# Two layers of attention and gated mixing on one core: transposes moved to transfers, VectorE's exponentials rebuilt from two addends

## The chip, the core and the metric

The kernel runs on one core of a Trainium2 chip. Five engines work side by side, each through its own list of instructions in order: TensorE (PE in the profile, with PEld for the loading of its weights), VectorE (DVE), ScalarE (ACT), GpSimd (POOL) and SyncE (SP), which here only issues transfers. They meet at semaphores. Matrix products land in PSUM, eight banks of 128 x 512 float32; everything else lives in SBUF, 128 partitions wide. The metric is the time on the device in microseconds (us), the median of several runs.

## The reference

Two identical layers are applied to x, 2048 tokens by 512 channels in bfloat16:

```python
x = x + attention(layernorm(x))
x = x + mixer(layernorm(x))
```

Attention has 32 query heads of 16 channels and one shared key and value head: `softmax(q k^T / 4) v`, then a 512 x 512 output product. The scores of one layer are 32 x 2048 x 2048 numbers, and each goes through an exponential. The mixer computes `z = gelu(x w_in)`, 1792 channels wide, keeps the first half as z1, normalises the second half to z2, mixes z2 over tokens with the 2048 x 2048 matrix `w_sp`, adds a bias per token, multiplies by z1 and applies `w_out`. `w_sp` is needed transposed, with source tokens on the partitions.

## The kernel before, in words

The 2048 tokens are 16 tiles of 128. Attention is cut into 32 groups per layer (`GROUPS`): two token tiles with 16 heads, or, for the last two tiles, one tile with 32 heads. A group goes over the 16 key tiles; one (group, key tile) pair is a unit. A unit has four blocks of 128 keys x 512 columns: four products on TensorE with 32 rows each (`scores`, L800) that can run beside each other. A layer has 512 units and so 2048 blocks.

Most units go to ScalarE. Their blocks fill two PSUM slots in turn, one of three banks and one of two (`push_slot`); one ScalarE instruction takes the exponential of a whole slot into the ring `P_ring` (L824), and TensorE multiplies each block by the values, with a column of ones for the softmax's sum (L841). All units of a group add up in one bank (`PVB`), which VectorE empties at the group's end (L926 to L935). The first two query tiles' four groups go over the keys piece by piece as these come (`attn_first`), the other 28 groups over all 16 key tiles at once (`attn_rest`).

Some units go to VectorE (`push_unit_dve`). It adds a bias to the scores, which are scaled to units of 1/128 of a binary exponent, clips them at zero and converts them to 16-bit integers (L872, four times a unit, 128 x 512 each). Read as bfloat16, such an integer is a power of two with a straight-line fraction. The error of that line is averaged away with five tables: the integers plus four constants (L881, four times a unit, 128 x 2048), and five weighted value products on TensorE (L887, five times four). `ON_DVE` gives three such units to each of 20 groups and two to each of 8, `FIRST_DVE` one to each of the first four groups: 80 a layer, 160 in all. The five tables of a unit lie in a ring of six tiles (`big`).

The order of every engine is made before the run by a planner (`_Graph.schedule`): each operation has a cost, a latency and a priority, and a simulated run picks what is ready. The result is one fixed list for each engine, the SP queue of transfers too. Where TensorE would lie idle the planner puts in products that add zero or write to a free bank (L631, L636, L639).

Three things are transposed before their products. Normalised tokens `xn` (`ln_tiles`) and attention outputs `o_norm` (`turn_o`, `turn_tile`) are turned on TensorE against an identity (L721, L945, L955) and copied out of PSUM by VectorE (L725, L948, L958). `w_sp` is read once at the start in 16 strips, turned on TensorE (L1272), copied (L1275) and written to a scratch tensor in HBM (`turn_wsp`); `mix_stage` and `mix_late` fetch pieces of it from there (L1154, L1189), 16 times a layer. The weights `wo`, `w_in`, `w_out` are loaded between these strips.

The mixing sums of early source tokens are formed during attention, in two stages, kept in HBM (`gp_scratch`) and read again. At the layer's end `mix_late` adds the last four source tiles, multiplies by z1 and applies `w_out`. At the change of layers the keys come in pieces of 2, 2, 4, 4 and 4 tiles (`KEYS`), each as soon as its tokens are done, and the first 16 units need only the first four key tiles. Three lines say what is queued in which way:

```python
def dma(fn, r, w, chan, us):
    return op("sp", fn, 0.7, r=r, w=w, prio=5, lat=us, chan=chan)
KEYS = ((0, 2), (2, 2), (4, 4), (8, 4), (12, 4))
```

Of the kernel before, what the change touches and what calls it, by code (L numbers as in the profile page):

```python
# [20 lines left out]
NF1 = 7  # L21
# [6 lines left out]
NPH = 5  # L28
PH_A = (0, 26, 51, 77, 102)
PH_W = (0.828125, 0.71875, 0.625, 0.54296875, 0.47460938)  # L30
Q_SCALE = 128.0 * 1.4426950408889634 * 0.25
E_SCALE = 0.6931471805599453 / 128.0
PH_BIAS = 127.0 * 128.0 - 128.0 * 2.102375911
# [7 lines left out]
BESIDE = 0.03  # L41

HOLDS = 2.5

# [31 lines left out]
class _Op:  # L76
    __slots__ = ("eng", "fn", "dur", "lat", "prio", "seq", "deps", "succ", "nleft", "chan", "chan_val",
                 "inc", "pos", "val", "clock", "t0", "task", "mode", "rows", "work", "opens", "nstart", "due", "chain")

    def __init__(self, eng, fn, dur, lat, prio, seq, chan, task, mode):  # L80
# [8 lines left out]
        self.lat = lat  # L89
        self.prio = prio  # L90
# [16 lines left out]
class _Graph:  # L107
# [66 lines left out]
    def schedule(self):  # L174
# [154 lines left out]
        while True:  # L329
            moved = True  # L330
            while moved:
                moved = False
                for e in ENGS:
                    if free[e]:
# [25 lines left out]
                        push(now + us + o.lat + SEM_LAT, 1, o)  # L360
                        at = now + us + o.lat + SEM_LAT
# [11 lines left out]
            while ev and ev[0][0] <= now + 1e-9:  # L373
                _, _, what, x = heapq.heappop(ev)
                if what == 0:
                    free[x] = True
                elif what == 1:
                    for s, k in x.succ:
                        if k == 1:
                            met(s, x)  # L380
                    t = x.task
                    if t is not None:
                        t.left -= 1
                        if t.left == 0:
                            for b in t.banks:
                                bank_free[b] = True
# [75 lines left out]
def bass_interleave_layers__grouped_kv_mqa__mixer_gmlp__prompt_kernel(  # L462
# [15 lines left out]
    P = 128  # L478
# [82 lines left out]
    z1flat = z1c[:].rearrange("p f s -> p (f s)")  # L561
    wsp_stage = z1flat[:, 0:2 * S].rearrange("p (b s) -> p b s", b=2)
    wsp_tile = z1flat[:, 2 * S:4 * S].rearrange("p (b t q) -> p b t q", b=2, q=P)
    Z1ALL = [("z1", f, t) for f in range(NF1) for t in range(NT)]

    wspT_d = nc.dram_tensor("wspt_scratch", [NT, P, S], BF16)
    wspT_dv = wspT_d.ap().rearrange("st p t -> p st t")
# [19 lines left out]
    def dma(fn, r, w, chan, us):  # L587
        return op("sp", fn, 0.7, r=r, w=w, prio=5, lat=us, chan=chan)

    def dve(fn, us, r, w, prio=5):  # L590
        return op("dve", fn, us, r=r, w=w, prio=prio)
# [73 lines left out]
    def load_weights(i):  # L665

        rd = [("wd", 2 * i + 1)]
        if i == 0:
            dma(lambda e: e.dma_start(wo_r[:], A_wo.rearrange("(c p) n -> p c n", p=P)), rd, ["wo"], "wo", 6.0)
        elif i == 1:  # L670
            dma(lambda e: e.dma_start(w_in_r[:], B_w_in.rearrange("(kd p) f -> p kd f", p=P)), rd, ["w_in"], "win", 10.0)
        elif i == 2:
            dma(lambda e: e.dma_start(w_out_r[:], B_w_out.rearrange("(c p) n -> p c n", p=P)), rd, ["w_out"], "wout",
                10.0)
# [29 lines left out]
    def ln_tiles(t0, n, xT, keys, per_tile, prio=5):  # L704
# [13 lines left out]
        while t < t0 + n:  # L718
            m = 1 if per_tile else min(2, t0 + n - t)
            tk = _Task()  # L720
# [3 lines left out]
            c0 = (t if xT is xnTA else t % CT) * P  # L724
# [78 lines left out]
    def push_slot(n):  # L803
# [22 lines left out]
        main["last"] = op("act", act_e, 0.065 + n * 0.4267, r=[tk], w=[("P", s0 + k) for k in range(n)], prio=3)  # L826
# [32 lines left out]
    def push_unit_dve(u):  # L859
# [3 lines left out]
        tiles = [phr["base"] + (phr["n"] + a) % phr["ring"] for a in range(NPH)]  # L863
        phr["n"] += NPH
        first_op = None
        for j in range(4):
# [7 lines left out]
                0.66, [tk], BIG(tiles[0]) if j == 0 else [("phj", tiles[0], j)], P_R)  # L874
# [5 lines left out]
        for a in range(1, NPH):  # L880
            dve(lambda e, a=a: e.tensor_scalar(ph16[:, tiles[a], :], ph16[:, tiles[0], :], float(PH_A[a]), None,  # L881
                                               op0=ALU.add), 0.63, base, BIG(tiles[a]), 4)
        for a in range(NPH):
# [484 lines left out]
```

## Time and profile before

| what | value |
|---|---|
| median of 3 runs | 1753.39 us (1752.82 to 1754.59) |
| span of the profiled execution | 1750.5 us |
| busy: PE, DVE, ACT, POOL | 1664.3, 1356.0, 1637.6, 90.4 us |
| ScalarE's exponentials (L824) | 1571.3 us for 3456 blocks in 1383 slots |
| first exponential of a layer | 13.63 us and 851.37 us |
| last exponential of a layer ends | 819.3 us and 1677.7 us |

The profile gives no duration for the profiled execution other than its span, which runs from the first to the last instruction; the median of the runs is 2.9 us above it. Each group of instructions is listed by line, engine, operation and shape, with how many there are, their busy time, the mean duration of one and the idle time of the engine just before them, with what ended it. Instructions of VectorE overlap at their ends, so a group's busy time divided by its count can be under its mean.

### The profile page before, as it was taken

Reading aid. Unit: us, or ns where it says so; the run is one execution under the profiler, and the core shown is the slowest. Engines: PE = TensorE matmul, PEld = TensorE weight load, DVE = VectorE, ACT = ScalarE, POOL = GpSimd, SP = SyncE. Lnnn points to the kernel's source line nnn. Section 1 sums busy time; section 2 is a strip of 40 time slices with the busy share of each in tenths; the row PEclk is TensorE's granted clock in tenths of the full one; section 3 lists DMA queues with packets and bytes.
Section 4 is the critical chain, followed back from the end, with each engine's and each line's share of the span. In section 5 each row is a group of like instructions: output and inputs, shape, how many; then the busy total and the mean of one; then the engine's idle time right before and its main releaser. Section 6 shows DMA issues by size and latency. Waiting matters only on the chain.

```text
span 1750.5 us, 44624 instructions
## 1 busy us (share of the span) xinstructions
PE 1664.3 (95%) x20010; PEld 579.3 (33%) x20010; DVE 1356.0 (77%) x2457; ACT 1637.6 (94%) x1425; POOL 90.4 (5%) x142
## 2 busy tenths in 40 slices
PE   8899999999999999999999999999999999999989
PEld 4332233332333333333432222333333333333334
DVE  8668788888877778675775987888888887766767
ACT  7999999999999999999659999999999999999970
POOL 2000000000000000000430000000000000000012
PEclk9999999999999999999999999999999999999999
DMA  6841000000100302335410000000000112033263
GB/s 185 225 103 49 1 1 2 1 2 25 41 14 20 106 23 70 124 96 161 144 53 19 2 2 1 2 1 2 7 26 7 53 46 88 15 110 110 98 224 120
DMA packets 94816, 104.22 MB, mean 60 GB/s; under 512 B 39072, under 2 KB 64288, under 8 KB 94624
## 3 DMA queue, kind: packets, MB, share of 16 engines
q1 hardware_dynamic: 94624, 101.37, 18.5%
q8 instruction: 156, 2.56, 0.6%
q14 instruction: 36, 0.29, 0.1%
HBM read 61.51 MB, written 39.85 MB: 58 GB/s over the span
## 4 chain that ended last, share of the span: by engine, by line
ACT 75%; PE 22%; DVE 1%; DMA 1%; issue 0%; SPq 0%; POOL 0%; DVEq 0%
ACT P_ring L824 73%; PE ps_all L613 6%; PE ps_all L800 6%; PE ps_all L618 4%; PE ps_all L841 3%; PE ps_all L887 2%; ACT z2n L1087 1%; PE ps_all L639 1%; ACT z1c L1115 0%; PE ps_all L721 0%; DVE big L1216 0%; DVE xn L714 0%; DMA X<-in_A_x_dram 0%; DVE big L1176 0%; DMA big<-gp_scratch 0%
## 5 line engine op out<-in xcount | busy, mean ns | idle before, releaser
L824 ACT ACTIVATE P_ring<-ps_all 128x1536 bf16<-128x1536 f32 (+1 forms) x1383 | 1571.3, 1325 | 56.5 <-PE ps_all L800 55.2
L800 PE MATMUL ps_all<-qT,kT_rep 32*128 32x512 bf16 x4096 | 637.5, 385 | 69.1 <-ACT P_ring L824 55.8
L872 DVE TENSOR_SCALAR big<-ps_all 128x512 int16<-128x512 f32 x640 | 421.8, 686 | 84.5 <-PE ps_all L800 80.2
L881 DVE TENSOR_SCALAR big<-big 128x2048 int16<-128x2048 int16 x640 | 416.2, 682 | 25.0 <-PE ps_all L887 23.8
L800 PEld LDWEIGHTS ps_all<-qT,kT_rep 32*128 32x128 bf16 x4096 | 159.1, 91 | 586.4 <-ACT P_ring L824 451.7
L841 PE MATMUL ps_all<-P_ring,V_aug 128*32 128x512 bf16 x3456 | 333.4, 389 | 0.8 <-DVE big L926 0.5
L887 PE MATMUL ps_all<-big,V_ph 128*32 128x512 bf16 x3200 | 265.0, 385 | 0.6 <-DVE big L872 0.4
L841 PEld LDWEIGHTS ps_all<-P_ring,V_aug 128*32 128x32 bf16 x3456 | 84.6, 93 | 180.7 <-issue 167.2
L639 PE MATMUL ps_all<-ones,zeros 128*32 128x512 bf16 x1320 | 115.0, 388 | 0.0
L887 PEld LDWEIGHTS ps_all<-big,V_ph 128*32 128x32 bf16 x3200 | 75.8, 95 | 90.5 <-issue 36.1
L613 PE MATMUL ps_all<-xnTA,z2n 128*32 128x512 bf16 x1344 | 92.5, 381 | 0.0
L697 POOL TENSOR_SCALAR ve<-mv 128x1 f32<-128x1 f32 (+3 forms) x40 | 10.6, 266 | 1577.3 <-DVE mv L710 1349.9
L962 DVE TENSOR_TENSOR X<-ps_all,X 128x512 bf16<-128x512 f32 x64 | 44.1, 688 | 40.0 <-PE ps_all L618 26.8
L935 DVE CAST oT<-ps_all 128x512 bf16<-128x512 f32 x56 | 38.7, 690 | 38.2 <-PE ps_all L841 38.0
L1176 DVE TENSOR_TENSOR big<-ps_all,big 128x512 f32<-128x512 f32 x56 | 38.3, 689 | 36.8 <-PE ps_all L613 36.5
L1176 DVE TENSOR_TENSOR big<-ps_all,bsp 128x512 f32<-128x512 f32 x56 | 38.5, 688 | 25.1 <-PE ps_all L613 24.6
L613 PE MATMUL ps_all<-w_in_r,xo 128*32 128x448 bf16 x960 | 57.3, 354 | 0.1
L618 PE MATMUL ps_all<-w_out_r,z1c 128*128 128x512 bf16 x224 | 54.2, 380 | 2.8 <-DVE z1c L1221 2.8
L1051 DVE CAST z2n<-ps_all 128x448 bf16<-128x448 f32 x60 | 37.4, 624 | 24.4 <-PE ps_all L613 22.6
L613 PE MATMUL ps_all<-xo,w_in_r 128*32 128x256 bf16 (+1 forms) x1120 | 52.4, 316 | 0.0
L618 PE MATMUL ps_all<-big,z2n 128*128 128x512 bf16 (+1 forms) x224 | 49.4, 366 | 1.3 <-DVE z2n L1131 1.3
L1077 DVE CAST z1c<-ps_all 128x512 bf16<-128x512 f32 (+2 forms) x56 | 36.6, 657 | 16.4 <-PE ps_all L613 13.6
(97 smaller groups left out, 1130.8 us busy)
## 6 DMA issues: line engine op xcount, KB each, us to landing
gp_scratch<-big SPq DMA_DIRECT2D x112, 256.0 KB, 2.0
big<-gp_scratch SPq DMA_DIRECT2D x105, 256.0 KB, 3.0
z1c<-in_B_w_sp_dram SPq DMA_DIRECT2D x16, 512.0 KB, 5.6
wspt_scratch<-z1c SPq DMA_DIRECT2D x16, 512.0 KB, 5.4
xnTA<-wspt_scratch SPq DMA_DIRECT2D x16, 384.0 KB, 4.1
big<-wspt_scratch SPq DMA_DIRECT2D x8, 512.0 KB, 5.8
z2n<-wspt_scratch SPq DMA_DIRECT2D x4, 768.0 KB, 4.8
z1c<-wspt_scratch SPq DMA_DIRECT2D x4, 768.0 KB, 5.6
```

The source lines that it names most:

```text
L613: ins = e.matmul(out_[32 * j:32 * j + 32, :], lhs[:, 32 * j:32 * j + 32], rhs, tile_position=(0, 32 * j), start=start, stop=stop)
L618: return e.matmul(out_, lhs, rhs, start=start, stop=stop)
L639: ins = e.matmul(bank32(PVB)[32 * j:32 * j + 32, :], zeros[:, 0:32], mv, tile_position=(0, 32 * j), start=False, stop=False)
L800: return e.matmul(out, kT_rep[32 * j:32 * j + 32, a, u[1] * P:(u[1] + 1) * P], qT[32 * j:32 * j + 32, q, :], tile_position=(32 * j, 0), st ...
L824: return e.activation(P_ring[:, s0:s0 + n, :], bank32(b0, n).rearrange("p (k q) -> p k q", k=n), ACTF.Exp, scale=E_SCALE)
L841: ins = e.matmul(bank32(PVB)[32 * j:32 * j + 32, :], V_aug[:, kt, :], P_ring[:, s, :], tile_position=(0, 32 * j), start=first, stop=last)
L872: o = dve(lambda e, j=j, tk=tk: e.tensor_scalar(ph16[:, tiles[0], j * QC:(j + 1) * QC], bank32(tk.bank), PH_BIAS, 0.0, op0=ALU.add, op1=AL ...
L881: dve(lambda e, a=a: e.tensor_scalar(ph16[:, tiles[a], :], ph16[:, tiles[0], :], float(PH_A[a]), None, op0=ALU.add), 0.63, base, BIG(tiles ...
L887: ins = e.matmul(bank32(PVB)[32 * j:32 * j + 32, :], V_ph[:, a, kt, :], big[:, tiles[a], j * QC:(j + 1) * QC], tile_position=(0, 32 * j), ...
L935: dve(lambda e: e.tensor_copy(oT[:, par, :], bank32(PVB)), 0.69, ["pvb"], [("oT", par)], 0)
L962: dve(lambda e: e.tensor_tensor(X[:, t, :], bank32(tk.bank), X[:, t, :], ALU.add), 0.69, [tk, ("X", t)], [("X", t)], prio)
L1176: dve(lambda e, part=part, tk=tk: e.tensor_tensor(part, bank32(tk.bank), part if st else bsp[:], ALU.add), 0.69, [tk] + ([] if st else ["b ...
```

## The change

- **Transposing transfers.** `dma_start_transpose`, issued by SP, takes the place of TensorE and VectorE for `w_sp` (straight from the input, whenever a piece is needed, so that the strips, the scratch tensor and its writes are gone), for `xn` except the tiles prepared one by one (the first four of each layer and the last) and those on the last group's chain, and for `o_norm` except the last tile. `turn_o` now runs once a token tile, after the tile's last group, and not once per pair of groups.
- **Two addends.** The integers of a unit are split: their exponent bits alone give 2^i, their fraction bits with exponent zero give 1+f, and the product of the integers read as bfloat16 with the latter gives 2^i (1+f)^2. The two addends are weighted 0.671875 and 0.330078125 in the value products. Per unit this is two bitwise operations and one multiplication of 128 x 2048 in place of four additions, and two times four value products in place of five times four. A unit holds three ring tiles.
- **More units on VectorE.** A table per layer and group, 100 units in the first layer and 94 in the second: 194 in place of 160. Three of `attn_first`'s key pieces hold one in the first layer, one in the second.
- **Planner.** VectorE operations get a latency of 0.085 us that is taken off their cost, ScalarE's a latency of 0.185, and a slot's banks count as free when the ScalarE instruction ends. SP's operations have a cost of their own. The weights are loaded at the start.

```diff
-NPH = 5
-PH_A = (0, 26, 51, 77, 102)
-PH_W = (0.828125, 0.71875, 0.625, 0.54296875, 0.47460938)
+NPH = 2
+PH_W = (0.671875, 0.330078125)
-PH_BIAS = 127.0 * 128.0 - 128.0 * 2.102375911
+PH_BIAS = 127.0 * 128.0
...
+DVE_LAT = 0.085
+ACT_LAT = 0.185
+UNITS = {0: (), 1: (4,), 2: (3, 8), 3: (2, 6, 10), 4: (2, 5, 8, 11), 5: (2, 4, 7, 9, 12)}
+FIRST_DVE = ({4: (2,), 8: (2,), 12: (2,)}, {12: (2,)})
+ON_DVE = ((0, 0, 0, 0, 3, 4, 5, 4, 3, 5, 2, 3, 5, 4, 4, 3, 3, 3, 4, 3, 3, 3, 2, 4, 2, 1, 1, 4, 2, 2, 2, 4),
+          (0, 0, 0, 0, 4, 3, 5, 4, 4, 3, 4, 4, 2, 2, 3, 4, 5, 4, 3, 4, 4, 2, 3, 3, 1, 4, 4, 2, 2, 3, 1, 3))
...
-    def dma(fn, r, w, chan, us):
-        return op("sp", fn, 0.7, r=r, w=w, prio=5, lat=us, chan=chan)
+    def dma(fn, r, w, chan, us, issue=0.7):
+        return op("sp", fn, issue, r=r, w=w, prio=5, lat=us, chan=chan)
     def dve(fn, us, r, w, prio=5):
-        return op("dve", fn, us, r=r, w=w, prio=prio)
+        return op("dve", fn, max(us - DVE_LAT, 0.06), r=r, w=w, prio=prio, lat=DVE_LAT)
...
+            if not per_tile and not G.chain:
+                m = 1
+                dma(lambda e, t=t, c0=c0: e.dma_start_transpose(xT[:, :, c0:c0 + P], xn[:, t % CT, :]),
+                    [("xn", t % CT)], keys(t), f"xt{t % CT}", 3.0, 1.3)
+                t += m
+                continue
...
-        for a in range(1, NPH):
-            dve(lambda e, a=a: e.tensor_scalar(ph16[:, tiles[a], :], ph16[:, tiles[0], :], float(PH_A[a]), None,
-                                               op0=ALU.add), 0.63, base, BIG(tiles[a]), 4)
-        for a in range(NPH):
+        bits = ph16[:, tiles[0], :]
+        dve(lambda e: e.tensor_scalar(ph16[:, tiles[1], :], bits, 0x7F80, None, op0=ALU.bitwise_and), 0.69, base,
+            BIG(tiles[1]), 4)
+        dve(lambda e: e.tensor_scalar(ph16[:, tiles[2], :], bits, 0x7F, 0x3F80, op0=ALU.bitwise_and,
+                                      op1=ALU.bitwise_or), 0.69, base, BIG(tiles[2]), 4)
+        dve(lambda e: e.tensor_tensor(big[:, tiles[2], :], big[:, tiles[0], :], big[:, tiles[2], :], ALU.mult), 1.22,
+            base + BIG(tiles[2]), BIG(tiles[2]), 4)
+        for a in range(2):
...
-    def turn_o(t0, n, c):
...
+    def turn_o(t):
+        i = t % CT
+        dma(lambda e: e.dma_start_transpose(xo[:, :, i * P:(i + 1) * P], o_norm[:, i, :]),
+            [("on", c, a, i) for c in range(4) for a in range(2)], [("xo", c, i) for c in range(4)], f"to{i}", 3.0, 1.3)
...
-    def turn_wsp(tt):
...
+    def turn_wsp(dst, s0, m, tc, keys, chan):
+        dma(lambda e: e.dma_start_transpose(dst, B_w_sp[tc * QC:(tc + 1) * QC, s0 * P:(s0 + m) * P]), [], keys, chan, 6.0,
+            1.2 + 0.45 * m)
```

## The prediction, made before the changed kernel ran

> **What bounds the kernel now.** First the page's busy times and slices, to see which engine is full.
>
> ```profile
> PE 1664.3 (95%) x20010; PEld 579.3 (33%) x20010; DVE 1356.0 (77%) x2457; ACT 1637.6 (94%) x1425; POOL 90.4 (5%) x142
> ...
> DVE  8668788888877778675775987888888887766767
> ACT  7999999999999999999659999999999999999970
> ```
>
> ScalarE is at nine tenths or more in nearly every slice and has only three holes: the start, the change of layers, the end. TensorE's 95% is not all work, as the groups below show. The chain that ended last agrees:
>
> ```profile
> ACT 75%; PE 22%; DVE 1%; DMA 1%; issue 0%; SPq 0%; POOL 0%; DVEq 0%
> ```
>
> Then busy times of the five stretches, cut at the first and last exponentials of each layer (columns: window, its length, busy PE, PEld, DVE, ACT, POOL, clock, DMA share, GB/s):
>
> ```profile
> 13.60:819.30 805.70, 766.58 (x9602) 263.07 (x9605) 627.69 (x1138) 799.24 (x698) 15.49 (x26) 1.00 0.20 60
> 819.30:898.00 78.70, 74.87 (x647) 34.25 (x640) 62.11 (x120) 47.11 (x40) 31.55 (x41) 1.00 0.43 134
> 898.00:1677.70 779.70, 748.19 (x9260) 247.99 (x9262) 604.39 (x1086) 772.57 (x673) 17.55 (x28) 1.00 0.12 39
> 1677.70:1750.50 72.80, 64.30 (x405) 28.80 (x397) 53.88 (x91) 17.41 (x15) 17.86 (x18) 1.00 0.47 155
> ```
>
> In both long stretches ScalarE is 99% busy (idle 6.5 and 7.1 us) and VectorE 78%. So a block that leaves ScalarE shortens them, as long as VectorE can take it. Last the groups that the change touches, and a piece of VectorE's timeline:
>
> ```profile
> L824 ACT ACTIVATE P_ring<-ps_all 128x1536 bf16<-128x1536 f32 (+1 forms) x1383 | 1571.3, 1325 | 56.5 <-PE ps_all L800 55.2
> ...
> L872 DVE TENSOR_SCALAR big<-ps_all 128x512 int16<-128x512 f32 x640 | 421.8, 686 | 84.5 <-PE ps_all L800 80.2
> L881 DVE TENSOR_SCALAR big<-big 128x2048 int16<-128x2048 int16 x640 | 416.2, 682 | 25.0 <-PE ps_all L887 23.8
> ...
> L887 PE MATMUL ps_all<-big,V_ph 128*32 128x512 bf16 x3200 | 265.0, 385 | 0.6 <-DVE big L872 0.4
> ...
> L639 PE MATMUL ps_all<-ones,zeros 128*32 128x512 bf16 x1320 | 115.0, 388 | 0.0
> ...
> L935 DVE CAST oT<-ps_all 128x512 bf16<-128x512 f32 x56 | 38.7, 690 | 38.2 <-PE ps_all L841 38.0
> ...
> L1051 DVE CAST z2n<-ps_all 128x448 bf16<-128x448 f32 x60 | 37.4, 624 | 24.4 <-PE ps_all L613 22.6
> ...
> L1275 DVE COPY z1c<-ps_all 128x1024 bf16<-128x1024 bf16 x32 | 21.8, 689 | 15.0 <-PE ps_all L1272 11.6 <-DMA wspt_scratch<-z1c 3.0
> ...
> L948 DVE COPY xo<-ps_all 128x256 bf16<-128x256 bf16 x56 | 15.6, 287 | 5.7 <-PE ps_all L945 4.8
> ```
>
> **The change part by part.** The sum is made against the profiled span, 1750.5 us; the median of the runs, 1753.39, is 2.9 above it, which I add at the end.
>
> *ScalarE's units.* 1571.3 us over 3456 blocks are 0.4547 us a block, 1.819 a unit. 34 units (20 in the first layer, 14 in the second) leave it: 136 blocks, **-61.8 us**, -36.4 and -25.5 by layer. All of it lies on the path while ScalarE stays full.
>
> *VectorE's units.* Before: four conversions at 421.8/640 = 0.659 and four additions at 416.2/640 = 0.650, 5.24 us; 160 of them are 838. After: four conversions (2.64), two bitwise operations, one multiplication. Neither of the latter is in the trace. The bitwise ones lie between 0.65 (the addition, same shape, type and place) and 2.27 (one element at a time: the casts of 448 and 512 float32 take 0.624 and 0.690, so 1.03 ns an element); I take 0.65, the row they match in everything but the operator. The multiplication has the same ends. The 16-bit copies of 256 and 1024 take 0.287 and 0.689, 0.523 ns an element, which gives 1.22 for 2048; I take that, as all its operands have 16 bits but, unlike the addition, there are two inputs. A unit is then 2.64 + 1.30 + 1.22 = 5.16, and 194 are 1001: +163 us.
>
> Taken off VectorE: L1275 whole (21.8), L948 whole (15.6), 12 of L725's pairs into xnTA and 16 into xo (8.3 and 10.3), half of L958 and of the weighted values L756 (2.5): -58.5. The net is +104 and a total of 1460. By stretch: 627.7 - 418.5 (80 units by their busy time there) + 516 - 38 = 687 in 805.7 - 36.4 = 769 us, 89%; 604.4 - 419.5 + 485 - 20 = 650 in 754, 86%. The fullest 50 us of the trace where ScalarE was full (1300 to 1350: 49.55) had VectorE at 44.07, 88%. Holding 88% would stretch the first layer's 687 to 781, 12 over; so VectorE's lateness costs 0 to 12. I take **+5**.
>
> *TensorE.* The value products of VectorE's units go from 3200 to 1552 (-136 at 0.083), ScalarE's fall by 136 (-13), the transposes of L1272, L721 and L945 mostly go (-52). Off the path, since 144 us of it is padding (L639 115.0, L631 20.9, L636 8.3); the planner's list fills 804 more of the L639 kind (+70). What it can give back is ScalarE's 13.6 us of small waits in the long stretches: 0 to -13.6. I take **-4**.
>
> *Transposing transfers.* Of `xn` 54, of `o_norm` 30, of `w_sp` 32, all on SP, in order with the gp loads and stores. No row shows one. The plain transfers of 128 KB:
>
> ```profile
> out_dram<-X SPq DMA_DIRECT2D x16, 128.0 KB, 1.7
> ...
> big<-gp_scratch SPq DMA_DIRECT2D x14, 128.0 KB, 3.1
> ...
> bsp<-in_B_b_sp_dram SPq DMA_DIRECT2D x8, 128.0 KB, 3.9
> ```
>
> At the start tiles 4 to 7 are normalised by 27.8 us and needed when 16 units are through, 13.6 + 16 x 1.819 = 42.7; the weights, `w_sp`'s first two pieces (768 KB, 5 us when plain) and these go ahead in the queue, and fit. The strips' traffic (DMA share 0.88 from 50 to 100 us) goes. Costed at 0, covered by these 15 us.
>
> At the change of layers there is no cover:
>
> ```profile
> 851.37 1.02 ACT L824 ACTIVATE P_ring<-ps_all 128x1024 bf16<-128x1024 f32 x1 [13.39 <-PE ps_all L800]
> ...
> 898.07 1.02 ACT L824 ACTIVATE P_ring<-ps_all 128x1024 bf16<-128x1024 f32 x1 [16.71 <-PE ps_all L800]
> ```
>
> ScalarE waits 16.7 us at 898 for keys 4 to 7. Their last `xn` was written at 893.9 and their key product began at 895.8: 1.9 us for transposes and copies. Through a transfer it is issue (0.3 plain, 1.3 by the planner's cost) and landing (1.7 to 3.9, or 5.8 if the four go like one of 512 KB): +0.1 to +5.2. I take **+3**. Behind the waiting product on TensorE stand this stretch's mixing products and the scores, so ScalarE waits with it.
>
> In the tail the second quarter's `w_sp` piece is issued at 1698.0, when its bank tiles come free, and used at 1709.0; plain it lands after 5.8, with 5 us to spare. Twice as slow plus a 3.0 issue, with five gp loads queued behind, it would cost 4: 0 to +4, I take **0**.
>
> Sum: -61.8 + 5 - 4 + 3 = -57.8, a span of 1692.7 and a time of **1696 us**; the ends of the terms (-75.4 and -40.6) give 1678 to 1713.
>
> The Trainium skill speaks against this part: "VectorE: DVE Perf Modes", section "The three transpose paths", has 390 ns for a 128 x 128 block on TensorE and 1309 ns by transfer. By that alone, an estimate: sixteen blocks one after another take 21 us, and the sum would be some 16 us higher, at 1712; for the rival of late transfers below it is 5.2 us a tile, one over the planner's 4.3. The trace's own side of it is 0.62 us for eight blocks on TensorE; no row here shows the other.
>
> **The rivals.**
>
> *VectorE becomes the bound in the first layer* (faster, but less). Three groups of its table hold five units, 25.8 us of VectorE against 11 x 1.819 = 20.0 of ScalarE. Against it: ring tiles now hold two units, and the planner can shift other work. If only 86% is reached, 687 becomes 799 (+30) and 650 becomes 756 (+2), in place of the +5 above: 1723; at 84%, +49 and +20, all is gone.
>
> *Transfers land later than the order assumes* (slower). Their consumers stand in TensorE's fixed list: a layer has 3 key pieces, 8 ends of query pieces and 6 fronts, 34 in all. A late one holds the scores behind it, and ScalarE has two slots ahead, five blocks or 2.27 us. The gain is gone when each costs 1.7 us, that is, when data come about 4 us later than the planner's 1.3 + 3.0. At 5 us late: 34 x 2.7 = 92, 1696 + 92 - 3 = 1785. For it: no transpose was measured; against it, 128 KB land within 3.9.
>
> *The multiplication or the bitwise operations run one element at a time* (slower). The multiplication alone at 2.27: +204 on VectorE, 792 and 749 us of work in stretches of 769 and 754; at 88% these become 900 and 851: +228, 1924. All three slow is beyond 2100. Even at 95% it is 834 + 788, +99: 1795.
>
> *More comes back*: the 30 us of waits at the change of layers also shrink as TensorE's list gets shorter: 1665 to 1678.
>
> *No change*: the gain and a loss cancel within 0.2%.
>
> **How the numbers follow.** The likeliest case 0.62 (1678 to 1713), VectorE bound 0.14 (1713 to 1745), more back 0.08, no change 0.03, late transfers 0.08, slow operations 0.05. About 0.2% (3.5 us) is what a measurement can tell from none. Faster 0.62 + 0.13 + 0.08 = 0.83, same 0.03 and 0.01 of the VectorE case, slower 0.13. The range runs from 1676 to 1742: 0.06 below, 0.14 above.
>
> **What would show it.** ScalarE's exponentials at 3320 x 0.4547 = 1510 us, and still above 98% busy in both long stretches; bitwise groups with a mean of 0.68 us and the multiplication near 1.25; VectorE at 86% of the span; ScalarE's second wait at the change of layers near 20 us; transposes landing within 4 us. I am wrong if the multiplication's mean is over 2 us, or if ScalarE's list of waits names score products behind transfers.

## The result, and the profile after

The changed kernel takes 1725.79 us (median of 4 runs, 1724.48 to 1731.93), the kernel before, beside it, 1753.99 (1752.82 to 1755.08): a ratio of 0.984, 95% interval 0.982 to 0.987. That is 28 us faster where 58 were forecast; it lies inside the range, 30 us from the predicted 1696. The profiled execution is the slowest of the four, 1731.93 us with a span of 1730.1.

From the page after: busy times, the slices of three engines and of TensorE's granted clock (tenths; before, the clock's row was 9 in all forty), and the chain that ended last.

```profile
PE 1614.2 (93%) x18419; PEld 535.9 (31%) x18419; DVE 1432.5 (83%) x2417; ACT 1581.7 (91%) x1370; POOL 94.8 (5%) x136
...
DVE  7989999899987775767666899997899985787677
ACT  5999999999999999999659999999999999799970
...
PEclk7989999999999999999998999999999999799999
...
ACT 68%; PE 24%; DVE 4%; SPq 2%; issue 1%; POOL 1%; DMA 0%; DVEq 0%
```

ScalarE's share of the chain fell from 75% to 68%, TensorE's rose from 22% to 24% and VectorE's from 1% to 4%; the clock has dents that it did not have. The stretches, cut as before at the first and last exponentials of each layer (length, busy PE, PEld, DVE, ACT, POOL, clock, DMA share, GB/s):

```profile
13.64:801.23 787.59, 736.57 (x8759) 236.72 (x8763) 667.40 (x1120) 766.19 (x665) 17.15 (x26) 0.97 0.19 48
801.23:885.13 83.90, 78.20 (x625) 35.70 (x614) 63.70 (x123) 47.36 (x41) 32.46 (x41) 0.98 0.45 121
885.13:1659.02 773.89, 724.90 (x8513) 229.50 (x8515) 636.45 (x1057) 749.46 (x650) 20.57 (x27) 0.96 0.17 44
1659.02:1730.10 71.08, 64.27 (x430) 28.61 (x418) 55.13 (x93) 17.39 (x14) 18.38 (x18) 1.00 0.60 170
```

The long stretches gained 18.1 and 5.8 us in place of 36.4 and 25.5. ScalarE's busy time fell nearly as forecast (by 33.0 and 23.1), but its idle time rose from 6.5 and 7.1 us to 21.4 and 24.4. The groups that answer to those shown of before:

```profile
L824 ACT ACTIVATE P_ring<-ps_all 128x1024 bf16<-128x1024 f32 (+1 forms) x1328 | 1515.1, 1324 | 93.5 <-PE ps_all L800 91.6
...
L874 DVE TENSOR_SCALAR big<-ps_all 128x512 int16<-128x512 f32 x776 | 507.5, 683 | 59.4 <-PE ps_all L800 55.9
...
L887 DVE TENSOR_TENSOR big<-big 128x2048 bf16<-128x2048 bf16 x194 | 234.7, 1210 | 0.7
L640 PE MATMUL ps_all<-ones,zeros 128*32 128x512 bf16 x2124 | 188.4, 401 | 0.0
L893 PE MATMUL ps_all<-big,V_ph 128*32 128x512 bf16 x1552 | 141.5, 397 | 1.4 <-DVE big L883 0.9
L883 DVE TENSOR_SCALAR big<-big 128x2048 int16<-128x2048 int16 x194 | 131.8, 679 | 12.2 <-PE ps_all L893 11.1
...
L885 DVE TENSOR_SCALAR big<-big 128x2048 int16<-128x2048 int16 x194 | 131.7, 679 | 0.0
```

The new operations cost what was forecast. ScalarE's waits for score products rose from 55.2 us to 91.6. Where they lie is seen around 100 us (windows of the trace, columns as above; then ScalarE's timeline: start, duration, instruction, wait before it):

```profile
90.00:98.00 8.00, 6.61 (x63) 1.88 (x59) 7.60 (x13) 8.00 (x8) 0.00 (x0) 0.97 0.00 0
98.00:111.00 13.00, 13.00 (x87) 2.94 (x84) 8.60 (x14) 9.56 (x9) 0.00 (x0) 0.50 0.01 2
111.00:119.00 8.00, 6.40 (x72) 2.10 (x68) 8.00 (x15) 8.00 (x8) 0.00 (x0) 0.99 0.00 0
```

```profile
100.36 1.02 ACT L824 ACTIVATE P_ring<-ps_all 128x1024 bf16<-128x1024 f32 x1 [0.39 <-PE ps_all L800]
102.74 2.53 ACT L824 ACTIVATE P_ring<-ps_all 128x1536 bf16<-128x1536 f32 x2 [1.35 <-PE ps_all L800]
105.77 2.37 ACT L824 ACTIVATE P_ring<-ps_all 128x1536 bf16<-128x1536 f32 x2 [0.50 <-PE ps_all L800]
```

For 13 us the clock stands at 0.50: TensorE is busy all the time and does 87 products, ScalarE is 9.56 us busy. In the windows before and behind it the clock is full (the first touches the spell with its last half microsecond), VectorE is fuller, 95 and 100% for 66%, and ScalarE has no gap. TensorE's own list shows how it began and what stood in front of the late scores:

```profile
95.51 0.39 PE L800 MATMUL ps_all<-qT,kT_rep 32*128 32x512 bf16 x3 [0.34 <-ACT P_ring L824]
95.83 0.61 PE L843 MATMUL ps_all<-P_ring,V_aug 128*32 128x512 bf16 x8
96.38 0.58 PE L800 MATMUL ps_all<-qT,kT_rep 32*128 32x512 bf16 x4
97.77 0.61 PE L800 MATMUL ps_all<-qT,kT_rep 32*128 32x512 bf16 x3 [0.81 <-ACT P_ring L824]
...
100.25 1.90 PE L640 MATMUL ps_all<-ones,zeros 128*32 128x512 bf16 x16
102.08 1.04 PE L800 MATMUL ps_all<-qT,kT_rep 32*128 32x512 bf16 x5
```

TensorE twice waits for a slot that ScalarE still holds, with nothing else to do; within the second of these waits, at 97.6 us, the clock is halved; then sixteen padding products, planned for an idle TensorE, hold up the scores by 1.9 us.

I sorted all of ScalarE's waits of 0.25 to 6 us before an exponential (15 to 1700 us) by the mean clock of the wait and the 1.5 us ahead of it. Before: 3.4 us at a clock under 0.98 and 8.5 at full clock. After: 30.9 and 12.3. TensorE ran at half clock for 11 us before and 123 after.

### The profile page after: what moved, and what is told of

It is laid out like the page before. It is cut to its first block, busy times and chain, and to the rows that moved or that the text cites. A ratio compares the mean times of both kernels' runs of the same rounds, so it can differ in the third digit from the quotient of the medians.

```text
span 1730.1 us, 41473 instructions
## 1 busy us (share of the span) xinstructions
PE 1614.2 (93%) x18419; PEld 535.9 (31%) x18419; DVE 1432.5 (83%) x2417; ACT 1581.7 (91%) x1370; POOL 94.8 (5%) x136
## 4 chain that ended last, share of the span: by engine, by line
ACT 68%; PE 24%; DVE 4%; SPq 2%; issue 1%; POOL 1%; DMA 0%; DVEq 0%
ACT P_ring L824 67%; PE ps_all L800 7%; PE ps_all L614 6%; PE ps_all L619 4%; PE ps_all L843 3%; PE ps_all L640 1%; SPq L1267 1%; PE ps_all L893 1%; ACT z2n L1089 1%; DVE st L1126 1%; SPq L653 0%; DVE big L1215 0%; POOL rs L693 0%; DVE st L703 0%; DVE xn L708 0%
## 5 line engine op out<-in xcount | busy, mean ns | idle before, releaser
L824 ACT ACTIVATE P_ring<-ps_all 128x1024 bf16<-128x1024 f32 (+1 forms) x1328 | 1515.1, 1324 | 93.5 <-PE ps_all L800 91.6
L800 PE MATMUL ps_all<-qT,kT_rep 32*128 32x512 bf16 x4096 | 660.6, 396 | 92.5 <-ACT P_ring L824 76.3
L874 DVE TENSOR_SCALAR big<-ps_all 128x512 int16<-128x512 f32 x776 | 507.5, 683 | 59.4 <-PE ps_all L800 55.9
L800 PEld LDWEIGHTS ps_all<-qT,kT_rep 32*128 32x128 bf16 x4096 | 165.0, 91 | 627.4 <-ACT P_ring L824 451.3
L843 PE MATMUL ps_all<-P_ring,V_aug 128*32 128x512 bf16 x3320 | 323.0, 399 | 4.2 <-DVE big L929 2.5
L887 DVE TENSOR_TENSOR big<-big 128x2048 bf16<-128x2048 bf16 x194 | 234.7, 1210 | 0.7
L640 PE MATMUL ps_all<-ones,zeros 128*32 128x512 bf16 x2124 | 188.4, 401 | 0.0
L893 PE MATMUL ps_all<-big,V_ph 128*32 128x512 bf16 x1552 | 141.5, 397 | 1.4 <-DVE big L883 0.9
L883 DVE TENSOR_SCALAR big<-big 128x2048 int16<-128x2048 int16 x194 | 131.8, 679 | 12.2 <-PE ps_all L893 11.1
L885 DVE TENSOR_SCALAR big<-big 128x2048 int16<-128x2048 int16 x194 | 131.7, 679 | 0.0
L640 PEld LDWEIGHTS ps_all<-ones,zeros 128*32 128x32 bf16 x2124 | 48.4, 96 | 83.7 <-issue 75.5
L964 DVE TENSOR_TENSOR X<-ps_all,X 128x512 bf16<-128x512 f32 x64 | 43.6, 683 | 30.8 <-PE ps_all L619 27.1
L893 PEld LDWEIGHTS ps_all<-big,V_ph 128*32 128x32 bf16 x1552 | 39.4, 96 | 53.7 <-issue 22.5
L619 PE MATMUL ps_all<-big,z2n 128*128 128x512 bf16 (+1 forms) x224 | 50.3, 371 | 5.2 <-DVE big L1215 3.2
## 6 DMA issues: line engine op xcount, KB each, us to landing
w_in_r<-in_B_w_in_dram SPq DMA_DIRECT2D x1, 1792.0 KB, 13.4
```

Source lines behind the costliest of these rows:

```text
L619: return e.matmul(out_, lhs, rhs, start=start, stop=stop)
L640: ins = e.matmul(bank32(PVB)[32 * j:32 * j + 32, :], zeros[:, 0:32], mv, tile_position=(0, 32 * j), start=False, stop=False)
L800: return e.matmul(out, kT_rep[32 * j:32 * j + 32, a, u[1] * P:(u[1] + 1) * P], qT[32 * j:32 * j + 32, q, :], tile_position=(32 * j, 0), st ...
L824: return e.activation(P_ring[:, s0:s0 + n, :], bank32(b0, n).rearrange("p (k q) -> p k q", k=n), ACTF.Exp, scale=E_SCALE)
L843: ins = e.matmul(bank32(PVB)[32 * j:32 * j + 32, :], V_aug[:, kt, :], P_ring[:, s, :], tile_position=(0, 32 * j), start=first, stop=last)
L874: o = dve(lambda e, j=j, tk=tk: e.tensor_scalar(ph16[:, tiles[0], j * QC:(j + 1) * QC], bank32(tk.bank), PH_BIAS, 0.0, op0=ALU.add, op1=AL ...
```

## The experiments

Theory A: gaps in TensorE's work lead to half-clock spells, in which ScalarE waits for scores. Rival B: VectorE is too full and what it feeds comes late. Rival C: the transposing transfers come late. The table has all runs; "half, full" are the waits just defined, "change" is ScalarE's open time at the change of layers (window less busy time; before 31.7, after 36.5), and the ratio is to the kernel before on the same chip. Times are medians; clock and waits are those of the one profiled execution, which in the changed kernel, e1 and e8 is the slowest, 6, 7 and 9 us over the median.

| run | edit | us | ratio, 95% | clock | half, full | change |
|---|---|---|---|---|---|---|
| before | | 1753.99 | 1 | 0.997 | 3.4, 8.5 | 31.7 |
| after | | 1725.79 | 0.982-0.987 | 0.964 | 30.9, 12.3 | 36.5 |
| e1 | more padding | 1723.03 | 0.981-0.985 | 0.988 | 15.6, 11.9 | 48.8 |
| e2 | 160 units | 1763.28 | 1.004-1.008 | 0.983 | 12.4, 7.1 | 36.0 |
| e3 | before + units | 1821.0 | 1.038-1.042 | 0.984 | 20.8, 50.3 | 26.6 |
| e4 | before + transfers | 1740.35 | 0.991-0.996 | 0.995 | 5.4, 5.8 | 25.9 |
| e5 | zero products | 1729.14 | 0.985-0.990 | 0.982 | 19.1, 15.4 | 36.6 |
| e6 | before, thin padding | 1800.58 | 1.025-1.029 | 0.946 | 37.8, 8.3 | 33.2 |
| e7 | old costs | 1798.35 | 1.023-1.027 | 0.984 | 19.3, 48.1 | 34.1 |
| e8 | keys on TensorE | 1715.35 | 0.976-0.982 | 0.977 | 23.3, 11.0 | 31.3 |
| e9 | e8 + padding in long stretches | 1707.44 | 0.971-0.977 | 0.995 | 3.8, 11.4 | 33.9 |
| e10 | e2 + old costs | 1751.9 | 0.998-1.001 | 0.985 | 13.5, 7.3 | 26.6 |
| e11 | ScalarE's old cost | 1714.76 | 0.976-0.980 | 0.986 | 15.7, 11.2 | 36.1 |
| e12 | before + new costs | 1766.13 | 1.005-1.009 | 0.986 | 13.4, 10.6 | 29.6 |
| e13 | e9 + e11 | 1710.71 | 0.972-0.976 | 0.991 | 6.0, 18.2 | 31.2 |
| e14 | e3 + new costs | 1767.39 | 1.005-1.009 | 0.968 | 31.1, 18.8 | 35.0 |
| e15 | padding in long stretches | 1725.12 | 0.981-0.985 | 0.994 | 6.3, 18.4 | 50.1 |
| e16 | e8 + padding, first parts | 1713.63 | 0.975-0.980 | 0.993 | 5.0, 20.8 | 41.1 |
| e17 | padding, first parts | 1721.77 | 0.981-0.984 | 0.991 | 8.5, 11.3 | 47.2 |

Waits of over 6 us in the long stretches are not in these columns: six in e3 (73.7 us) and five in e7 (53.6), one of 13.8 in e14, and one of 6.7 to 9.4 in e1, e9, e15, e16 and e17, all at full clock. The last five are one and the same, to which I come back.

### The clock: e1, e5, e6

e1 raises the planner's threshold for padding:

```diff
-WARM = 0.55
+WARM = 0.75
```

> The changed kernel with one constant altered: the planner pads TensorE up to 75% of a 3.4 us window in place of 55%. Theory A (TensorE, emptied of value products and transposes, is halved in clock for about 13 us after each gap, and ScalarE then waits for scores): the mean granted clock rises from 0.964-0.973 to at least 0.985, ScalarE's idle time in the two long stretches falls from 45.8 us to 15-25 us, and the time from 1726 to 1695-1708 us. Rival B (VectorE is too full and what it feeds comes late): padding does nothing for VectorE, ScalarE's idle time stays above 40 us and the time is 1720-1735. Rival C (the transposing transfers come late): the same as B.

The clock rose and the waits at half clock halved, as theory A has it, but ScalarE's idle time in the long stretches fell only from 45.8 to 37.4 us, between the numbers of A and of B, and the time is that of B and C: the change of layers had 12.3 us more of open time. Theory A was right on the spells and wrong on what padding would bring; this is taken up below.

e5 leaves every list as it is and gives each VectorE unit one set of products that add zero:

```diff
+                if a == 0:
+                    ins = add_zeros(e, 2)
```

> The changed kernel, every engine's list as it is, except that each VectorE unit's first value product is followed by one more set of four products that add zero: 194 sets, 776 products, about 70 us of TensorE's time put back out of the 149 us that the change took from its value products. Theory A (half-clock spells follow gaps in TensorE's work; 31.8 us of ScalarE's waits in the changed kernel lie at half clock, 4.5 in the kernel before): the waits at half clock fall to 10-18 us although TensorE has more to do, and the time falls to 1708-1718. Rival D (TensorE is simply too busy when VectorE's products come in bursts): more products make it worse, 1735-1760.

Half-clock time fell from 123 to 61 us and the waits in it by 12, but the waits at full clock rose by 3 and the median is not shorter (the profiled executions have spans of 1726.7 and 1730.1). It neither bears out theory A's number nor rival D's.

e6 goes at it from the other side, in the kernel before:

```diff
-            return e.matmul(bank32(PVB), zeros[:], mv, start=False, stop=False)
+            return e.matmul(bank32(PVB)[:, 0:64], zeros[:], ones[:, 0:64], start=False, stop=False)
...
-            ins = e.matmul(bank32(PVB)[32 * j:32 * j + 32, :], zeros[:, 0:32], mv, ...
+            ins = e.matmul(bank32(PVB)[32 * j:32 * j + 32, 0:64], zeros[:, 0:32], ones[:, 0:64], ...
```

> The kernel before with every engine's list as it is, but its padding products (added zeros, about 123 us) cut from 512 columns to 64, so that nearly no time is spent in them. Theory A: what kept the clock up is gone; the mean granted clock falls from 1.00 to 0.93-0.97, ScalarE's waits at half clock rise from 4.5 us to 25-60, and the time rises by 20-50 us to 1775-1805. Rival D (TensorE's load is what counts): 123 us less of it, so ScalarE's waits fall, if anything, and the time is 1745-1755.

From its page (clock by slices) and its groups (the padding):

```profile
PEclk9899899889998898999998988999899999999999
```

```profile
L639 PE MATMUL ps_all<-ones,zeros 128*32 128x64 bf16 x1320 | 54.7, 207 | 0.0
```

60 us of padding fewer (54.7 in place of 115.0), and 47 us more in all: 195 us at half clock, 37.8 us of waits in them, no more waits at full clock than before. TensorE's busy time rose from 1664.3 to 1679.6 us, with less to do. The lists are the same but for the padding's width, and all engines but TensorE have the work that they had. This is the run that shows the cause: less work on TensorE, a lower clock, late scores. It shows it in the kernel before; what the spells cost in the changed kernel it does not say.

### Units, transfers, planner: e2, e3, e4, e7, e10, e11, e12, e14

e2 puts the old tables of units into the changed kernel; e10 takes the planner's old costs too.

> The changed kernel with the old numbers of units on VectorE (80 a layer; transfers, two addends and planner kept). 136 blocks go back to ScalarE, 61.8 us by 0.4547 us a block; VectorE loses 34 units of 5.16 us, 175 us. Rival B (VectorE too full): ScalarE's idle time of 45.8 us in the long stretches falls to about 14, the time is 1726 + 62 - 30 = 1750-1760. Theory A: TensorE's real work per ScalarE block is no larger than in the changed kernel, the half-clock spells stay, and the time is 1775-1790. Rival C: 1780-1790.

> The changed kernel with 80 units a layer and the planner's costs of before: transfers and two addends. Transfers alone (five tables, old costs) took 1740, transfers with two addends and the new costs 1763. If the new costs make the difference, this run takes 1738-1748. If it is the two addends, which leave TensorE emptier, it takes 1755-1768 at a clock of 0.985 or less.

e2's time lies between the numbers of B and A. ScalarE's exponentials took 56.5 us more (1571.6), and the profiled span is 30.3 us longer (1760.4). Most of the other 26 are waits: outside the first 60 us, 3.9 us at half clock are left of 23.8. So rival B has a part: without VectorE's 34 extra units most of the spells behind the start do not come. But its fullness alone stops nothing. These windows of the changed kernel have VectorE at 97 to 99% and ScalarE without a gap, at full clock:

```profile
200.00:225.00 25.00, 23.13 (x274) 7.55 (x272) 24.58 (x42) 25.00 (x23) 0.00 (x0) 1.00 0.06 12
225.00:250.00 25.00, 23.00 (x255) 6.71 (x253) 24.18 (x43) 24.95 (x23) 2.43 (x2) 1.00 0.15 22
250.00:275.00 25.00, 23.48 (x280) 7.39 (x278) 24.82 (x40) 25.00 (x23) 0.00 (x0) 1.00 0.01 2
```

e10 fell between its two numbers. Against e4, which differs from it in having the five tables, it has 12 us more, a clock of 0.985 for 0.995 and 8 us more of half-clock waits: a cheaper TensorE made a slower kernel. Its ten runs fall in steps with the clock: 1756.5 us at 0.982, 1751.8 to 1753.8 at 0.985, 1747.6 to 1748.5 at 0.988 and 0.989.

e3 and e4 add one part each to the kernel before, with its planner costs.

> The kernel before with the two addends and the 194 units alone; transposes stay on TensorE and VectorE, the planner's costs are those of before. VectorE has its transposes' 58 us more than in the changed kernel: about 745 us of work in the first layer where ScalarE needs 769. Rival B: VectorE is the bound in the first layer, 93% at most, so that the first layer gains nothing, and the time is 1735-1755. Theory A: TensorE keeps 52 us of transposes, so fewer half-clock spells than in the changed kernel, clock 0.97-0.99; the time is 1705-1725 if that is what held the changed kernel.

> The kernel before with the transposing transfers (and the early weight loads) alone; five tables, 160 units and the planner's costs of before. Nothing leaves ScalarE, so no gain is expected. Theory A: TensorE loses only 52 us of 1664, few spells; the start costs about 7 us and the change of layers 5: 1754 + 12 = 1760-1770, ScalarE's idle time in the two long stretches 20-27 us (7 of them at the start). Rival C (transfers are what ate the gain): ScalarE's idle time as in the changed kernel, 40 us or more, and 1775-1790.

Both missed their numbers. e4's gain is not the transfers' doing as far as I can show: its change of layers (25.9 us open) and its end (65.5 us after the last exponential, before 72.8) are those of e3 and e10 as well, of which e3 has no transfers. e3 was far slower, which the next runs explain.

> The changed kernel with the planner's costs of before (no latency taken off VectorE's operations, ScalarE's banks freed as before). Transfers alone with those costs had 25.9 us of ScalarE's time open at the change of layers (36.5 in the changed kernel) and 65.5 us after the last exponential (71.1). If that comes from the planner's costs, the time is 1705-1715; if the transfers or the 160 units brought it, 1722-1730. If the old costs make VectorE's list fall behind with 194 units, as in units alone, it is 1740 or more, with waits of over 5 us in the long stretches.

> The changed kernel with one half of the planner's costs of before: ScalarE's slot counts as free only after its latency and its cost is as before; VectorE's new latency stays. With both halves undone it took 1798. If VectorE's half keeps its list from falling behind, this run has no wait over 5 us in the long stretches (apart from that of 3.9 us near 1510) and takes 1720-1740; if ScalarE's half does, it takes 1775-1800.

> The kernel before with the planner's new costs alone: five tables, 160 units, transposes on TensorE. If these costs are better in themselves, ScalarE's waits at the change of layers and the time after its last exponential shrink and the time is 1735-1748; if they only pay when VectorE has 194 units, 1750-1765. Theory A: TensorE's work is that of before, so the clock stays above 0.99.

e7 takes both new costs out of the changed kernel and loses 72 us; e11 takes only ScalarE's and gains 11. The third case of e7's expectation holds. TensorE's timeline in e7 ahead of ScalarE's wait of 16.30 us at 292.42:

```profile
285.21 0.40 PE L800 MATMUL ps_all<-qT,kT_rep 32*128 32x512 bf16 x4
285.54 2.13 PE L640 MATMUL ps_all<-ones,zeros 128*32 128x512 bf16 x36
289.07 0.40 PE L891 MATMUL ps_all<-big,V_ph 128*32 128x512 bf16 x4 [1.40 <-DVE big L881]
289.30 1.68 PE L640 MATMUL ps_all<-ones,zeros 128*32 128x512 bf16 x28
291.41 0.40 PE L891 MATMUL ps_all<-big,V_ph 128*32 128x512 bf16 x4 [0.43 <-DVE big L885]
291.63 0.39 PE L841 MATMUL ps_all<-P_ring,V_aug 128*32 128x512 bf16 x4
291.95 0.61 PE L800 MATMUL ps_all<-qT,kT_rep 32*128 32x512 bf16 x7
```

ScalarE's scores (L800, 291.95) stand in TensorE's fixed list behind value products whose tables VectorE has only just made (waits of 1.40 and 0.43 us), and behind 64 padding products. VectorE's latency in the planner is what keeps its list in step with 194 units. ScalarE's is not needed: without it the changed kernel is faster (1714.76), and the new costs in the kernel before cost 13 us (e12, just above both of its numbers). e12's clock is 0.986 to 0.992 over its runs, where theory A had it above 0.99, and in the profiled one 13.4 us of waits lie at half clock: a new order alone, with TensorE's products those of before, brings spells too.

> The kernel before with 194 units, two addends and the planner's new costs, but all transposes on TensorE and VectorE (58 us more on VectorE). With the old costs it took 1821. If the transfers' relief of VectorE carries the 194 units, VectorE needs 715 us in the first layer and at the 89% which units alone and the changed kernel at most held over a layer (85% in the changed kernel) it takes 805 or more: 1750-1780. If it was the planner's costs alone that failed there, it takes 1720-1740.

The units need the transfers too: without them, and with the new costs, 1767, as the first case has it. VectorE has 704 us of work in a first layer of 815 us, 28 longer than in the changed kernel, and there are 31 us of waits at half clock, as many as there. The end takes 88.6 us for 71.0; why, I did not follow.

### The queue at the start and at the change of layers: e8

```diff
-            if not per_tile and not G.chain:
+            if not per_tile and not G.chain and not (xT is xnTA and t0 == 4):
```

> The changed kernel with the second key piece's tokens (tiles 4 to 7, both layers) transposed on TensorE and copied by VectorE as before; all other transfers stay. If the queue of transfers holds the second key piece, ScalarE's 7.1 us of waits between 15 and 50 us fall to 1-3, and its wait at the change of layers from 22.5 to 17-20, the time to 1715-1720. If the waits at the start come from the half-clock spell alone they stay at 5-7 us; if the change of layers is held by the mixing products ahead in TensorE's list, its wait stays at 22.

Ten us faster, and each number of the first case came true. Between 15 and 50 us ScalarE is busy 35.00 us before, 27.92 after and 32.96 here. At the change of layers, windows and wait in e8:

```profile
802.84:881.70 78.86, 73.09 (x603) 33.48 (x596) 62.27 (x119) 47.53 (x42) 32.79 (x42) 1.00 0.49 123
```

```profile
881.70 1.02 ACT L824 ACTIVATE P_ring<-ps_all 128x1024 bf16<-128x1024 f32 x1 [17.33 <-PE ps_all L800]
```

78.86 us for 83.90, and 17.33 us of wait for 22.47. In the profiled execution the first layer as a whole took no less, as spells between 76 and 175 us came in place of those at the start, the second layer's long stretch took 14.3 us less, and the end 9.8 more (80.8).

### Why padding alone did not pay: e9, e13, e15, e16, e17

e9, e13 and e15 pad to 75% only in the long stretches, e16 and e17 only in the part of each where VectorE is full:

```diff
+            warm = 0.75 if 45.0 < now < 740.0 or 880.0 < now < 1580.0 else WARM
-            if have >= WARM * WARM_US:
+            if have >= warm * WARM_US:
```

> The changed kernel with tiles 4 to 7 transposed on TensorE as in the run with the keys on TensorE (1715 us, granted clock 0.977 to 0.986, 23.3 us of ScalarE's waits at half clock), and with TensorE padded up to 75% in place of 55%, but in the two long stretches alone, so that start, change of layers and end keep their padding. Theory A: clock at least 0.990, waits at half clock under 12 us, 1700-1708. If padding only moves the waits from half clock to full clock, as it partly did when it was raised everywhere: 1712-1722.

> The changed kernel with 75% padding in the two long stretches alone; start, change of layers and end keep 55%. Theory A: the change of layers stays at 84 us (it took 96 where padding was raised everywhere), waits at half clock in the long stretches fall from 24.7 us to under 8, the clock is at least 0.985, and the time 1708-1716. If padding pays only with the keys on TensorE, 1720-1728.

> The changed kernel with the keys of tiles 4 to 7 on TensorE, 75% padding in the two long stretches, and ScalarE's half of the planner's costs of before. The first two alone gave 1707, the third alone 1715 (changed kernel 1726). If the third has a cause of its own its 11 us add up: 1693-1700. If it only led to fewer half-clock spells (waits at half clock 15.7 us with it, 3.8 us already gone to with keys and padding), nothing is left to gain: 1703-1711.

e9 is the fastest kernel here, 45.6 us under the kernel before and 18 under the changed one. Its windows:

```profile
13.82:788.11 774.29, 754.55 (x9485) 247.78 (x9489) 671.48 (x1123) 764.74 (x665) 19.05 (x26) 0.99 0.19 48
788.11:869.09 80.98, 75.86 (x628) 35.17 (x621) 62.99 (x120) 47.10 (x41) 33.71 (x42) 0.98 0.44 123
869.09:1632.17 763.08, 750.85 (x9415) 246.21 (x9418) 639.13 (x1060) 746.56 (x650) 20.23 (x26) 1.00 0.18 46
```

With VectorE as full as after (671 us for 667), 13.3 and 10.8 us are gone from the long stretches. e13 shows that e11's gain does not add to this, as its second case has it: it was, it seems, another way to fewer spells. One long wait of e9, at full clock, is in no column of the table (ScalarE, then TensorE):

```profile
1486.95 3.71 ACT L825 ACTIVATE P_ring<-ps_all 128x1536 bf16<-128x1536 f32 x3 [9.42 <-PE ps_all L801]
```

```profile
1478.63 4.50 PE L615 MATMUL ps_all<-z2n 128*32 128x512 bf16 x80
1482.96 2.76 PE L615 MATMUL ps_all<-xnTA,z2n 128*32 128x512 bf16 x48
```

128 mixing products stand ahead of the scores in TensorE's list. The same wait took 3.9 us in the changed kernel (1513.6), 7.8 in e1, and 6.7 in e15, e16 and e17. e15, without the keys on TensorE, shortened the long stretches by 12.8 us in all, but its change of layers took 92.3 us. There I saw more mixing products left over (into `ps_all` from `xnTA` and `z2n`, 144 in place of 116 between 800 and 890 us) and supposed that padding where TensorE is full had put them off.

> As the run with keys on TensorE and 75% padding in the long stretches (1707), but padded so only in the part of each stretch in which VectorE is full and TensorE is not (about 45 to 490 us and 890 to 1410 us); the rest keeps 55%. If padding in the rest displaced real work, the change of layers stays at 79-81 us, the 9.4 us wait near 1487 us goes, and the time is 1695-1705. If the rest needs the padding too, spells come back after 500 and 1400 us and the time is 1707-1713.

> The changed kernel with 75% padding in those two parts alone; keys by transfer as in the changed kernel. If the padding of the full parts was what lengthened the change of layers to 92 us, it is back at 82-86 us, the gain of the long stretches (12.8 us) stays for the most part, and the time is 1710-1718. If the keys by transfer are what keeps padding from paying, 1722-1727.

That supposition fell: with hardly more padding there than in the changed kernel (272 products between 500 and 800 us for 248), e17 has a change of layers of 94.6 us, and long stretches 20.6 us shorter. e16's change grew too, from e8's 78.9 to 89.0 us. e17's time lies at the edge of its second case, e16's just above both of its numbers.

What the lengths go with is how many of these mixing products each list leaves between the last exponential of the first layer and the end of ScalarE's second wait. There are 44 in e13, 68 in e8, 92 in e9 and 100 in the changed kernel, whose changes take 78.3, 78.9, 81.0 and 83.9 us. There are 160 in e15, 200 in e16, 220 in e17 and 228 in e1, which take 92.3, 89.0, 94.6 and 96.1. These four spend 11.0 to 14.9 us on them, the changed kernel 6.1. Under a hundred the count seems to decide little (e11 has none and takes 83.1). So four lists with more padding left work to the change of layers, and those of e9 and e13 did not; why the planner put it there is not shown.

## Why the prediction was wrong, by its own steps

In the profiled span the forecast was 1692.7 and the measurement 1730.1, 37.4 us more. Some 6 of these are this execution's own: the other three had spans of 1722.6 to 1724.8, at a clock of 0.971 to 0.973.

- *ScalarE's units, -61.8*: right but for 5.5. 3320 blocks took 1515.1 us, 0.4564 each for 0.4547; in e6, where only TensorE's padding differs, they also grow, by 6.5 us.
- *VectorE's units*: right. 679 ns for the bitwise operations (680 forecast), 1210 for the multiplication (1220), 83% of the span (86%).
- *VectorE's lateness, +5 from a ceiling of 88%*: there is no such ceiling. VectorE stood at 97 to 99% over 75 us with ScalarE full, and before the change it had 94% with ScalarE full from 970 to 1020 us (columns as above), so that 1300 to 1350 was not the fullest stretch:

```profile
970.00:1020.00 50.00, 47.30 (x579) 15.12 (x575) 47.18 (x88) 49.77 (x45) 0.00 (x0) 1.00 0.01 1
```

The rival "VectorE becomes the bound" gave 1723, nearly the time measured, for a reason that does not hold: e9 has VectorE at 671 us of work, the changed kernel at 667, in a first layer 13 us shorter. That the time fell where this rival had it is luck.
- *TensorE, -4*: **the step that failed.** It took value products and transposes as work "off the path", so that a shorter list could give back small waits, 0 to -13.6, and could cost nothing. But TensorE's gaps halved its clock, and waits at half clock rose by 27.5 us, 7.1 of them before 50 us. The term's parts add up to 131 us less work; TensorE's busy time fell by 50.1. The padding that was counted as free time is what held the clock, as e6 shows with 47 us in the kernel before. The planner's 804 more of it (2124 for 1320) stand where its plan had gaps, which need not be where the chip has them, and in a spell they hold up the scores. How much of the 27.5 the spells themselves cost is open. e9, with keys on TensorE, has 27.1 us fewer of these waits and takes 18 us less; e15 has 24.6 fewer and takes the same time, as other waits grew. And the emptier TensorE is not the only source of gaps: the units (e2) and the planner's new costs (e11, e12) each have a part.
- *Transposes at the start, 0*: wrong by 5.5. ScalarE waited 7.1 us before 50 us, and 1.6 with the keys of tiles 4 to 7 on TensorE (e8). The 15 us of cover were counted to the moment when the units run out, but other work stood behind the transfers earlier. On SP's timeline (start, duration of the issue), the two `w_sp` pieces, queued behind the weights, held SP for 18 us. The keys' tokens were written by 24.65 us and their first transpose was issued at 28.03; their key product, ahead of scores in TensorE's list, began at 34.51, before at 32.52:

```profile
8.85 13.24 SPq L1267 DMA_TRANSPOSE z2n<-in_B_w_sp_dram  x1
22.14 0.57 SPq L1158 DMA_DIRECT2D bsp<-in_B_b_sp_dram  x1
22.75 5.23 SPq L1267 DMA_TRANSPOSE z1c<-in_B_w_sp_dram  x1
28.03 17.55 SPq L717 DMA_TRANSPOSE xnTA<-xn  x12
```

VectorE's next tile of tokens had to wait until a transpose had read the old one, and TensorE waited for what stood behind it in VectorE's list; the clock was halved from 32.7 us, for 13.7 us:

```profile
31.05 0.41 DVE L708 TENSOR_SCALAR xn<-X,mv,rs 128x512 bf16<-128x512 bf16 x1 [3.16 <-DMA xnTA<-xn]
32.30 0.40 PE L843 MATMUL ps_all<-P_ring,V_aug 128*32 128x512 bf16 x4 [2.22 <-DVE big L929]
```

- *Change of layers, +3 (0.1 to 5.2)*: right, at its upper end: the window grew by 5.1, and by nothing in e8.
- *Tail, 0*: 1.7 us better.
- *Late transfers*: not so, but for the start: VectorE waited 4.2 us in all for transposes and TensorE 0.7, both there. Of the 128 x 512 tiles the median landed after 2.5 us, of the `w_sp` pieces after 4.1 or 5.2. From the profile's table of transfers (tile, queue, kind, count, median us from issue to landing):

```profile
xo<-o_norm SPq DMA_TRANSPOSE x30, 2.5
xo<-xn SPq DMA_TRANSPOSE x30, 2.5
xnTA<-xn SPq DMA_TRANSPOSE x24, 2.5
xnTA<-in_B_w_sp_dram SPq DMA_TRANSPOSE x16, 4.1
```

- *The planner's costs*: the sum had no term for them. VectorE's latency carries 194 units (e11 against e7: 84 us), ScalarE's cost 11 us in the changed kernel.

The sum of what was missed: 27.5 at half clock, 3.8 at full clock, 5.5 for slower blocks, 2.1 at the change of layers, -1.7 at the end, 37.2, less the net +1 that the terms of VectorE and TensorE had: 36.2 of the 37.4. The start's 5.5 are inside the 27.5, and the 3.8 at full clock are as large as the wait at 1513.6 us behind the mixing products. This sum sorts the waits that were measured; it does not show that each would be saved.

## What to carry to other kernels

Work taken off an engine that is not the bound is not free where that engine's speed depends on its being busy: price what its gaps do, and look at the granted clock by slices before costing them at nothing. Padding that a plan places is part of the kernel; when the plan's work shrinks, the padding has to be looked at anew, and with it what else the new order moves: here long waits and left-over work at the change of layers took back what fewer spells gave. A change of a planner's costs needs a term of its own in the sum.

## What the runs showed of the hardware

Spells of half clock last whole multiples of 3.4 us: in the changed kernel fifteen, of 3.4, 6.8, 13.7, 17.1 and 20.5 us. One, at 875.8 us, came at the end of a pause of 3.24 us. Ahead of the other fourteen TensorE was 40 to 94% busy over 4 us; ahead of 97.5 us it was 72% busy, with 0.81 us as its longest wait. Nor does full work end a spell at once: from 98 to 111 TensorE was busy all the time and stayed at 0.50.

The Trainium skill's page "TensorE: Matmul & The Clock Gate", section "Part 1: The HAM clock gate", has the clock set over windows of about 3.4 us, halved after at least one idle window and full again after a busy one. The trace agrees on the length of the window and not on the other two: before 97.5 us no window was idle, and then four went by at 0.50 that the profile, whose ends of products are modelled, shows as busy. The Trainium skill's section "A second HAM failure mode: psum-queue depth-cycling" on the same page speaks of short idle times between groups of products that are enough to make the clock swing, and that is what these traces show.

The Trainium skill's page "VectorE: DVE Perf Modes", section "The three transpose paths", gives 1309 ns for a 128 x 128 block transposed by transfer, which had put the sum 16 us higher. The trace has a tile of four blocks landing 2.5 us after issue, 0.6 us a block; at the change of layers four such tiles were issued within 5.12 us, 0.32 us a block. What the trace has against these transfers is the hold on the queue: SP took 13.24 us over the issue of one `w_sp` piece at the start.
